# A sparse attention and maxout kernel: emission order from a list scheduler inside the kernel, key tiles in token order, and a first batch masked by matmul

## The chip, the cores, the metric

The kernel runs on one NeuronCore of a Trainium2 chip. The metric is device time in microseconds (us) of one execution; the span of a profile is 1.6 to 2.7 us shorter in these runs, since it goes from the first to the last instruction. The engines are named as in the profile: PE is TensorE (PEld its weight loads), DVE is VectorE, ACT is ScalarE, POOL is GpSimd, SP is SyncE, which here issues the DMAs. A "q" behind an engine's name is its sequencer.

## The reference

Inputs q, k and v are float32 of shape (4, 8, 768, 64): 4 batches, 8 heads, 768 tokens, 64 dims. Cut to what matters:

```python
block, window = 32, 16
k_sum = k.reshape(B, H, nb, block, D).max(axis=3)      # 24 block maxima of k
v_sum = v.reshape(B, H, nb, block, D).mean(axis=3)     # 24 block means of v
scores_l = where(|i - j| < window, scale * q @ k.T, -1e9)
scores_s = scale * q @ k_sum.T + log(block)
a = softmax(concat(scores_l, scores_s))
attn = a @ concat(v, v_sum)
x = attn as (3072 tokens, 512)                          # heads side by side
h1, h2 = x @ w1, x @ w2                                 # 512 -> 1024
out = maximum(h1, h2) @ w_out                           # 1024 -> 512, float32
```

Both kernels use max(h1, h2) = h1 + relu(h2 - h1). So they need `wd = w2 - w1`, and fold the h1 part into `w1o = w1 @ w_out`. No output can be computed before w1o exists, and w1o needs all of w1 and w_out.

## The kernel before

Keys are taken in 12 tiles of 64 queries: 96 nearby keys and the 24 block sums make the 120 rows of one score matmul. Two heads share a matmul (a "head pair"). Cuts are marked with `...`.

```python
def load_pair(src, b, hp, tag):            # k, q or v of two heads: runs of 2 tokens = 512 bytes
    t = stage.tile([128, 6, 128], F32, tag=tag, bufs=3, name=tag)
    nc.sync.dma_start(out=t[:], in_=src[b, 2 * hp:2 * hp + 2].rearrange(
        "h (c p j) d -> p (h c) (j d)", p=128, j=2))
    return t

def prep_v(b):
    ...                                     # cast v to bf16: four DVE copies into vbt
    for j in range(2):
        r = j * 48
        nc.sync.dma_start(out=vx[r:r + 48, 0], in_=vbt[0:48, 0, j])
        ...                                 # 8 DMAs in each turn: rows of v to the key tiles
    ...                                     # matmuls with amean: block means, to vx[96:120, 0]
    nc.sync.dma_start(out=vx[96:NK, 1:NT]..., in_=vx[96:NK, 0:1] broadcast)   # the 17th

def attention(b):                           # a generator: yields between stages
    prep_kq(b, 0)
    yield
    for hp in range(NP):
        scores(b, hp, 0)
        yield
        ...
        values(b, hp, 2)
        yield

def maxout(b):                              # hidden layer in halves of 384 tokens, then output
    ...
            ps = psum.tile([128, d_model], F32, tag="o", bufs=1, name="o_ps")   # one bank
    ...

load_batch(0)
prep_v(0)
load_weights()
for _ in attention(0):
    pass
cast_weights()
make_w1o()
for b in range(B):
    side = iter(())
    if b + 1 < B:
        load_batch(b + 1)
        prep_v(b + 1)
        side = attention(b + 1)
    for _ in maxout(b):                     # one step of attention(b+1) per step of maxout(b)
        next(side, None)
    for _ in side:
        pass
```

The softmax here doesn't subtract the row's maximum and nothing guards it: scores larger than these inputs give would overflow.

## Time and profile before

| | before |
|---|---|
| median of three runs | 225.39 us (225.26 to 226.34) |
| span of the profile | 224.2 us |
| first hidden matmul (L330) | 40.2 us |
| first w1o matmul (L174) | 61.9 us |
| last matmul | 221 us |

First the page of the kernel before: busy time per engine, then the span in 40 slices of 5.6 us, where each digit is the busy share in tenths; PEclk is the granted clock of TensorE.

```profile
PE 174.6 (78%) x1475; PEld 103.8 (46%) x1496; DVE 118.0 (53%) x268; ACT 102.7 (46%) x173; POOL 23.9 (11%) x61
...
PE   0003832665788999896989999999999999999973
...
PEclk9999999997699999999999999999999999999999
DMA  6998438999997335999634599634431101202112
```

PE does nothing in the first three slices and little in the next nine. But "busy" is no measure of matmul work, since a record includes the time in which the matmul waits in the pipeline. The timeline of the dense end gives the real spacing:

```profile
207.00 4.24 PE L330 MATMUL h_ps<-xt,wd 128*128 128x384 bf16 x24
...
213.92 0.59 ACT L347 COPY osb<-o_ps 128x512 f32<-128x512 f32 x1 [2.14 <-PE o_ps L343]
214.55 1.02 PE L339 MATMUL o_ps<-w1o,xt 128*128 128x512 bf16 x4 [0.72 <-ACT osb L347]
```

In the chain of waits the same 24 matmuls take 4.08 us. From the starts of matmuls in such rows I take 216 ns for 512 columns, 163 ns for 384, 56 ns for 128 and 30 ns for the value matmuls, which have 65 (in undisturbed groups they start 30 ns apart in the mean). With one such spacing for each weight load (all 1,496 of them are in the trace), the necessary PE work can be summed by stretch. These sums are estimates; "lost" is the length of a stretch less its work.

| kernel before, us | length | PE work | lost |
|---|---|---|---|
| 0 to 40 | 40 | 5.0 | 35.0 |
| 40 to 75 | 35 | 20.5 | 14.5 |
| 75 to 130 | 55 | 47.8 | 7.2 |
| 130 to 190 | 60 | 55.2 | 4.8 |
| 190 to 221 | 31 | 27.8 | 3.2 |

49.5 of 64.7 lost us lie before 75 us. The tail's losses have a visible reason, in the row at 214.55 above: the output uses one PSUM bank, so PE waits 0.72 us for the copy.

The chain of waits shows why the fill, the time until PE has steady work, is long (columns: start, us, what the chain followed):

```profile
4.46 7.18 DMA vf<-in_v_dram
11.66 1.08 DVE vb_113 L182
12.74 0.55 SPq L127
13.38 6.33 DMA vf<-in_v_dram
19.74 0.57 DVE vb_113 L182
20.36 0.63 SPq L188
...
31.47 0.60 SPq L195
32.18 4.53 DMA vext_115<-vext_115
36.75 0.78 PE av L277 x11
```

v arrives last of three loads per pair, its last cast ends at 20.3 us, then SyncE is occupied by 17 small spreads (the DMAs that copy rows of v to the key tiles) until 33 us, and the first full value group runs at 36.75 us.

### The profile page before, as it was taken

The numbers are of one execution on the slowest core, as the hardware profiler recorded it, in microseconds if no ns is written. First come the engines' busy times: TensorE is split into PE (matmuls) and PEld (weight loads), VectorE is DVE, ScalarE is ACT, GpSimd is POOL, SyncE is SP. The second block draws the span as 40 slices with busy tenths as digits, with TensorE's granted clock in tenths as the row PEclk, the third lists the DMA queues.
The fourth block names the chain that finished last, engine by engine and source line by source line (L and its number), as shares of the span: only waits on it lengthen the run. The fifth ranks groups of instructions, "written<-read, shape, count | busy, mean of one in ns | idle before, by whom it ended". The sixth has DMA issues, their size and how long they took to land.

```text
span 224.2 us, 3831 instructions
## 1 busy us (share of the span) xinstructions
PE 174.6 (78%) x1475; PEld 103.8 (46%) x1496; DVE 118.0 (53%) x268; ACT 102.7 (46%) x173; POOL 23.9 (11%) x61
## 2 busy tenths in 40 slices
PE   0003832665788999896989999999999999999973
PEld 0001622543553655664555466655546664544531
DVE  5432852899972950896857069844727853000000
ACT  2000651575120573585179248824935972442521
POOL 8990110000000010000011001000000000000000
PEclk9999999997699999999999999999999999999999
DMA  6998438999997335999634599634431101202112
GB/s 187 289 290 273 106 100 251 375 365 283 288 281 183 90 90 135 288 292 282 184 117 102 158 259 306 163 116 152 103 87 50 51 0 47 96 0 95 47 47 94
DMA packets 49858, 37.68 MB, mean 168 GB/s; under 512 B 2192, under 2 KB 44720, under 8 KB 49840
## 3 DMA queue, kind: packets, MB, share of 16 engines
q1 hardware_dynamic: 49840, 37.45, 58.5%
q8 instruction: 11, 0.18, 0.3%
q14 instruction: 7, 0.06, 0.1%
HBM read 25.17 MB, written 6.29 MB: 140 GB/s over the span
## 4 chain that ended last, share of the span: by engine, by line
PE 49%; DMA 15%; DVE 13%; ACT 11%; SPq 7%; issue 3%; POOL 1%; ACTq 0%; POOLq 0%
PE o_ps L343 16%; DMA vf<-in_v_dram 13%; PE h_ps L330 11%; PE o_ps L339 8%; PE av L277 4%; PE sc L253 2%; ACT g L332 2%; PE x_ps L294 2%; DMA vext_115<-vext_115 2%; DVE wd L161 2%; SPq L127 2%; ACT qbd_107 L242 2%; PE vs_ps L199 2%; ACT qbd_108 L242 2%; PE w1o_ps L174 2%
## 5 line engine op out<-in xcount | busy, mean ns | idle before, releaser
L330 PE MATMUL h_ps<-xt,wd 128*128 128x384 bf16 x256 | 54.2, 331 | 2.5 <-DVE xt L296 1.1
L343 PE MATMUL o_ps<-wo,g 128*128 128x512 bf16 x186 | 46.5, 379 | 0.3
L332 ACT ACTIVATE g<-h_ps 128x384 bf16<-128x384 f32 x64 | 30.1, 491 | 15.7 <-PE h_ps L330 15.2
L347 ACT COPY osb<-o_ps 128x512 f32<-128x512 f32 x24 | 14.1, 586 | 49.2 <-PE o_ps L343 49.1
L330 PEld LDWEIGHTS <-wd 128*128 128x128 bf16 x256 | 23.7, 98 | 16.8 <-issue 3.0
L343 PEld LDWEIGHTS <-g 128*128 128x128 bf16 x192 | 17.9, 98 | 18.2
L339 PE MATMUL o_ps<-w1o,xt 128*128 128x512 bf16 x83 | 24.1, 378 | 2.1 <-ACT osb L347 1.4
L199 PE MATMUL vs_ps<-vb_113,amean 128*128 128x512 bf16 x12 | 4.2, 502 | 20.4 <-DVE vb_113 L182 20.4
L282 DVE RECIPROCAL inv<-av 128x6 f32<-128x6 f32 x32 | 6.1, 190 | 25.0 <-PE av L277 24.9
L284 DVE TENSOR_TENSOR x<-av,inv 128x384 bf16<-128x384 f32 x32 | 17.6, 550 | 0.3
L234 DVE TENSOR_REDUCE ks<-k_ps 128x24 bf16<-128x768 bf16 x16 | 15.1, 945 | 0.0
L162 ACT CAST wo<-wof 128x1024 bf16<-128x1024 f32 x4 | 4.2, 1043 | 23.8 <-DMA wof<-in_moe_w_out_dram 23.8
L339 PEld LDWEIGHTS <-xt 128*128 128x128 bf16 x96 | 9.1, 97 | 10.4 <-issue 4.0
L199 PEld LDWEIGHTS <-amean 128*128 128x128 bf16 x24 | 2.5, 107 | 24.3 <-issue 13.8
L296 DVE COPY xt<-x_ps 128x384 bf16<-128x384 bf16 x32 | 11.3, 352 | 2.8 <-PE x_ps L294 2.2
L294 PE MATMUL x_ps<-identity,x 128*128 128x128 bf16 x96 | 11.2, 230 | 1.4 <-ACT qbd_108 L242 0.6
L242 ACT COPY qbd_107<-q_ps 64x768 bf16<-64x768 bf16 x10 | 7.9, 792 | 9.3 <-PE q_ps L219 9.2
L255 ACT ACTIVATE prob_109<-sc,bias 120x512 bf16<-120x512 f32 x12 | 8.3, 689 | 7.8 <-PE av L277 6.7
L242 ACT COPY qbd_106<-q_ps 64x768 bf16<-64x768 bf16 x12 | 9.5, 793 | 4.0 <-PE q_ps L219 3.9
L213 DVE CAST qb<-qf 128x768 bf16<-128x768 f32 x16 | 10.3, 647 | 1.1 <-DMA qf<-in_q_dram 1.1
L182 DVE CAST vb_113<-vf 128x768 bf16<-128x768 f32 x8 | 5.1, 638 | 10.4 <-DMA vf<-in_v_dram 10.3
L219 PE MATMUL k_ps<-identity,kb 128*128 128x128 bf16 x96 | 9.8, 236 | 1.0 <-DVE ks L234 0.9
(94 smaller groups left out, 251.0 us busy)
## 6 DMA issues: line engine op xcount, KB each, us to landing
kf<-in_k_dram SPq DMA_DIRECT2D x16, 384.0 KB
qf<-in_q_dram SPq DMA_DIRECT2D x16, 384.0 KB
vf<-in_v_dram SPq DMA_DIRECT2D x16, 384.0 KB
out_dram<-osb SPq DMA_DIRECT2D x24, 256.0 KB
w1f<-in_moe_w_dram SPq DMA_DIRECT2D x4, 512.0 KB
wof<-in_moe_w_out_dram SPq DMA_DIRECT2D x4, 512.0 KB
w2f<-in_moe_w_dram SPq DMA_DIRECT2D x4, 512.0 KB
vext_115<-vb_113 SPq DMA_DIRECT2D x8, 148.5 KB
```

The source lines that it names most:

```text
L199: nc.tensor.matmul(out=ps[:], lhsT=amean[:, c, :], rhs=vbt[:, c, j, :, 0:D], start=(c == 0 and j == 0), stop=(c == 2 and j == 1))
L213: nc.vector.tensor_copy(out=qb[:], in_=by_slot(loads["qf", b, hp]))
L234: nc.vector.tensor_reduce(out=ks[:], in_=kps.rearrange("p j (n g) -> p n j g", g=16), axis=AX.XY, op=ALU.max)
L242: nc.scalar.copy(out=qx[r, :, a * 64:a * 64 + 64].rearrange("p t (g j) -> p t g j", j=2), in_=qps[r].rearrange("p j (t g) -> p t g j", g=32))
L284: nc.vector.tensor_tensor(out=x[:], in0=av[:, :, :, 0:D], in1=inv[:].to_broadcast([128, 3, 2, D]), op=ALU.mult)
L294: nc.tensor.transpose(out=ps[:, u, :], in_=xs[half][:, u].rearrange("p a d -> p (a d)"), identity=identity[:])
L296: nc.vector.tensor_copy(out=xts[b, half][:, hp, :], in_=ps[:].rearrange("p u n -> p (u n)"))
L330: nc.tensor.matmul(out=h[:], lhsT=wd[:, c, f * 128:f * 128 + 128], rhs=xt[:, c, :], start=(c == 0), stop=(c == KC - 1))
L332: nc.scalar.activation(out=g[:, f, :], in_=h[:], func=ACT.Relu)
L339: nc.tensor.matmul(out=ps[:], lhsT=xt[:, c, sl], rhs=w1o[:, c, :], start=(c == 0), stop=False)
L343: nc.tensor.matmul(out=ps[:], lhsT=g[:, f, sl], rhs=wo[:, f, :], start=False, stop=(f == FC - 1))
L347: nc.scalar.copy(out=o[:, u, :], in_=ps[:])
```

## The change

Its intent: every operation is declared with an engine, an assumed duration, the buffers that it reads and writes, and a priority. A small list scheduler simulates the engines, gives each operation its buffer slot and an order of emission, and the kernel is then emitted in just that order (manual scheduling). Beside this, the data layout is new: keys of a tile stand in token order with row groups of 64 + 32 sums + 32; k and q are loaded in runs of 6 tokens (1,536 bytes), v in runs of one (256 bytes); v is spread by 5 DMAs and one for the means in place of 16 and one; all PSUM banks form one pool; the hidden layer goes in groups of 256 tokens. Batch 0 is done group by group over all head pairs, and its mask is added by a matmul with the identity; GpSimd and ScalarE take the casts of batch 0.

The diff, cut to its core:

```diff
+class Ring:        # slots; find() returns a free slot at the modelled time
+class Buf:         # a buffer; its slot is given when its first writer is scheduled
+class Plan:
+    LAG = {"PE": 0.25, "ACT": 0.2, "DVE": 0.15, "POOL": 0.2, "SP": 2.0}
+    ISSUE, DEPTH = 0.55, 4
+    def op(self, engine, us, fn, read=(), write=(), change=(), touch=(), prio=0.0, label=""):
+        ...
+    def run(self):
+        ...                      # at each 0.02 us, each free engine takes its first ready task
+                if e == "SP":
+                    busy[e] = now + self.ISSUE
+                    t.done = max(sent[-1], now + 0.4) + t.us
+                    sent.append(t.done)
+                else:
+                    busy[e] = t.done = now + t.us
+        ...
+        for t in order:
+            t.fn()
...
+    banks = Ring(list(range(8)), {"kq": 2, "sc": 2, "av": 2, "mm": 3})
...
+            op("SP", 1.05, lambda f=f, src=src: nc.sync.dma_start(
+                out=f.ap[:], in_=src[b, 2 * hp:2 * hp + 2].rearrange("h (p j) d -> p h (j d)", j=J)),
...
+            op("SP", 3.45, lambda f=f, n=n: nc.sync.dma_start(
+                out=f.ap[:].rearrange("p h m d -> p (h m) d"),
+                in_=v[b, 4 * n:4 * n + 4].rearrange("h (m r) d -> r (h m) d", r=128)),
...                              # five spreads of v: 1.3, 1.3, 0.65, 0.6 and 0.2 us
+        op(engines[2], 1.2 if engines[2] == "SP" else 1.6, spread_means, read=[mean],
+           write=[vx[b]], prio=prio + 2, label=f"spread means {b}")
...
+            if mask_on == "PE":
+                for i in range(2):
+                    nc.tensor.matmul(out=view()[:, i], lhsT=identity[:], rhs=hide..., start=(i == 0), stop=False)
...
+    def first_attention():
+            prep(0, hp, hp, *FIRST[hp])
+            for grp in range(NG):
+                pbs[hp, grp] = scores(0, hp, grp, (10, 110, 210)[grp] + hp, "PE")
+        for grp in range(NG):
+            for hp in range(NP):
+                values(0, hp, grp, pbs[hp, grp], (20, 120, 220)[grp] + hp)
...
+    make_w1o(450)
+    for b in range(B):
+        for grp in range(NG):
+            maxout(b, grp, 1000 * b + 1500 + 10 * grp)     # attention(b) has 1000 * b
```

## The prediction

> **What bounds the kernel now.** TensorE, after a long fill. The page counts PE busy 174.6 of 224.2 us, yet a matmul's record includes waiting. The timeline's dense end gives real spacing: eight 512-column matmuls in 1.73 us (216 ns), four 384-column ones in 0.65 us (163 ns), eight score matmuls in 0.45 us (56 ns)[...]. This agrees with the Trainium skill, "TensorE: Matmul & The Clock Gate" (part 1: columns ÷ 2.4 GHz plus 2.5 ns). With the page's counts I estimate 160 us of necessary PE work: hidden 42, output 62, w1o 7, w1 transposes 2, block means 5, k/q transposes 11, scores 11, values 15, x transposes 5.
>
> Counted by stretch, only 26 us of that is done by 75 us: 49 us are lost in the fill. From there to the last matmul (221 us) 134 us of work take 146 us: 91% in the mixed stretch, then a tail where one output bank makes PE wait for the copy (0.7 us each). Copy and store take the last 3.5 us.
>
> Why the fill is long (timeline, chain of waits): SyncE issues in order. v loads come third (chain: "vf" 13%); PE idles to 20.4 us for the last v cast; then 17 small spreads hold the queue from 20.4 to 33 us, most weights are issued after that. Values wait for the spread until 36.75. wd appears at 38.6 to 56.5, w1o only after attention 0, at 62 to 75 us.
>
> **What the change does.** PE work hardly changes: masking by PE adds 24 matmuls of 256 columns (an estimate of 2.6 us). DVE loses 12 mask multiplies (0.43 us each) and batch 0's casts; POOL takes casts. k and q come in 1,536-byte runs, not 512; v in 256-byte runs, not 512: slower by the skill's "DMA: Bandwidth & Descriptors" (Specifications: line rate from 512 bytes). Spreads fall from 17 to 6 a batch. Eight PSUM banks are pooled. All is ordered by priority over modelled times.
>
> **Critical path.** Before w1o can start, DMA must bring batch 0 (4.7 MB), 1.2 MB of spreads and 6.3 MB of weights: 12.2 MB at an estimated 310 GB/s (before: slices of 290 with 512-byte rows, up to 375 with weights) is 39 us, so w1o starts near 42 us (before: 62). By then PE can have done attention 0, hidden 0 and w1 transposes: 26 us, so 16 us are lost in the fill: gain 33. Then 136 us remain at some 95%, since attention is preferred, maxout fills, and pure maxout ends it: 143 us against 146: about 4 gained. Tail unchanged.
>
> **Prediction: 188 us**, 178 to 203 in 8 of 10. Faster by over 2%: 0.93; within: 0.04; slower: 0.03.
>
> **What will show it.** Wd subtractions at about 22 to 38 us; first w1o matmul at 38 to 46 us; PE row at 9s from slice 10 (of 40); no long PE idle on v or DMA after 45 us; last 40 us dense at 216 ns without waits on the output copy.
>
> **What would make it wrong.** The order is fixed by modelled durations: if POOL's casts, the 256-byte v loads or the permuted PSUM copies are slower than modelled, in-order queues stall behind them, and the fill grows (200 and more). If dependencies on the shared PSUM tile are coarser than a bank, PE serializes with its evictions (slower than before). If PE holds 98% and batch 1 arrives in time, 178.

## The result, and the profile after

The kernel after takes 200.03 us (median of 4 runs, 199.25 to 200.78), against 225.32 us before (225.0 to 226.34). The ratio is 0.887, with a 95% interval of 0.8826 to 0.8915. Ratios are computed as the mean time of one kernel's runs over that of the other's in the same rounds, so they are not quite the ratio of the medians quoted. Executions over 1.5% slower than the fastest of the same kernel are left out of the means.

The page after, the same rows as before; a slice is 4.9 us here:

```profile
PE 170.1 (86%) x1664; PEld 119.9 (61%) x1664; DVE 104.8 (53%) x286; ACT 113.2 (57%) x173; POOL 25.0 (13%) x40
...
PE   0358629999999984999849999999999999999991
...
PEclk9999985999999996699999999999999999999999
DMA  6999999999999999999999995033020110311203
```

PE starts at 7.9 us and is full from slice 7 on (counted from 1), but for two dents (slices 15 and 16, and 20 and 21). The DMA row, which had gaps before, is full to slice 24, which ends at 118 us. The dense end no longer waits on a copy: each group of matmuls is followed by the next at once (their records overlap).

```profile
184.59 3.66 PE L548 MATMUL banks<-xt,wd 128*128 128x256 bf16 x32
...
188.08 1.89 PE L562 MATMUL banks<-w1o,xt 128*128 128x512 bf16 x8
...
189.81 3.62 PE L569 MATMUL banks<-wo,g 128*128 128x512 bf16 x16
```

The same accounting as before (value matmuls 30 ns each as there; a 256-column matmul 109 ns):

| kernel after, us | length | PE work | lost |
|---|---|---|---|
| 0 to 30 | 30 | 8.3 | 21.7 |
| 30 to 44.6 (first w1o matmul at 44.5) | 14.6 | 12.4 | 2.2 |
| 44.6 to 60 | 15.4 | 15.2 | 0.2 |
| 60 to 75 | 15 | 12.7 | 2.3 |
| 75 to 105 | 30 | 22.5 | 7.5 |
| 105 to 193.5 (last matmul) | 88.5 | 87.8 | 0.7 |

By 75 us the kernel after has lost 26.4 us, and before 49.5: this is 23 of the 27 us by which the span fell. From 75 us to the last matmul it lost 8.2 against 15.2: another 7. The sum of work rose from 156 to 159 us, mostly by the 24 masks. So the change gained by feeding PE earlier and more evenly, not by giving it less to do. The w1o matmuls, which open the way to all output, show the earlier start (count, ns min/median/max, first and last start; before, then after):

```profile
L174 PE MATMUL w1o_ps<-wo,w1t x30: 376/379/390, 61.9 to 74.8; 128*128 128x512 bf16 x30
```

```profile
L532 PE MATMUL banks<-wo,vx x32: 378/379/379, 44.5 to 52.1; 128*128 128x512 bf16 x32
```

Where the rest of the loss lies, the waits of PE tell (who waited for whom: us in all, times, longest):

```profile
PE banks L448 <- DMA vx<-vx: 9.0, 3, 3.3
PE banks L347 <- POOL kqb L328: 8.5, 2, 7.9
PE banks L402 <- DVE kx L370: 2.2, 1, 2.2
PE banks L448 <- DMA vx<-vb: 2.0, 1, 2.0
```

The second row is mostly the wait for the first k at the start. The first row is the DMA that copies the block means to the other eleven key tiles. It stops PE in batches 0, 1 and 2, as the timeline of PE shows (in brackets: idle before, and its releaser):

```profile
26.00 0.20 PE L448 MATMUL banks<-vx,pb 128*128 128x65 bf16 x1 [1.96 <-DMA vx<-vb]
28.68 0.98 PE L448 MATMUL banks<-vx,pb 128*128 128x65 bf16 x15 [2.47 <-DMA vx<-vx]
...
76.68 0.98 PE L448 MATMUL banks<-vx,pb 128*128 128x65 bf16 x15 [3.31 <-DMA vx<-vx]
...
101.33 0.39 PE L448 MATMUL banks<-vx,pb 128*128 128x65 bf16 x7 [3.24 <-DMA vx<-vx]
```

The first two stalls cost more than their length. The trace's clock records show half clock from 27.8 to 34.6 us and from 75.6 to 82.4 us, 6.8 us each. The Trainium skill ("TensorE: Matmul & The Clock Gate", part 1) states that PE falls to half clock after an idle window of some 3.4 us, and that these windows run freely, whatever the kernel does. The length agrees: half clock lasts multiples of 3.41 us in every trace, but for a last piece at the end. That the window must be idle throughout does not: in the window from 72.2 to 75.6 us, before the second half clock, PE was idle for 65%. Counted over all 14 traces, each of the 29 windows at full clock with 57% or more idle was followed by half clock, and none of the 619 with 46% or less; between the two both occur. The third stall, 3.24 us before 101.33, fell across two windows (41% and 54% idle) and was not followed by half clock: as to the clock, it had a lucky phase. A stall of 3.3 us at 73.4 us thus became a loss of about 6: 1.6 in the stretch to 75 us, and 4.3 from 75 to 90.

The plan itself, the modelled times in the kernel, can be laid beside the trace, as every PE task stands in the same order in both. The plan ends at 184.4 us, the chip's span at 197.4. The slip of PE against the plan is 1.5 us at the first values of batch 0, 4.3 behind the stall at 28.7, 4.3 to 6.0 from there to 73 us, 8.1 behind the stall at 76.7 and 10.6 behind the half clock, 13.1 behind the stall at 101.3. So, after the start, the plan was missed at three places, all of them arrivals of v, and behind two of them half clock added to the slip; from the last one on PE won back 2 us.

The DMA packets of both traces (each record has a size and a time) tell what changed in the queue's load. "Us of 16 engines" is the sum of the packets' times over 16; packets of one engine can overlap (the DMA share reaches 1.09 in some stretches), so this is a measure of load and not of time.

| packets | before: ns each, us of 16 engines | after: ns each, us of 16 engines |
|---|---|---|
| k and q | 512 B: 31.0, 47.6 | 1,536 B: 72.9, 37.3 |
| v | 512 B: 31.0, 23.8 | 256 B: 22.2, 34.1 |
| spreads of v and means, 1,056 B | 68.3, 24.2 | 85.8, 32.3 |
| w1 and w2 | 4,096 B: 178.9, 11.5 | 1,024 B: 52.8, 13.5 |
| w_out and output, 2,048 B | 89.3, 22.9 | 90.0, 23.0 |
| sum, the smallest packets included | 131.2 | 141.4 |

What k and q gain from long runs, v loses with short ones, and the spreads are dearer although they are fewer DMAs. In a fill where DMA is full, this is 10 us more of DMA work.

### The profile page after: what moved, and what is told of

The parts are those of the page before. It is cut to its first block, busy times and chain, and to the rows that moved or that the text cites. A ratio compares the mean times of both kernels' runs of the same rounds, so it can differ in the third digit from the quotient of the medians.

```text
span 197.4 us, 4172 instructions
## 1 busy us (share of the span) xinstructions
PE 170.1 (86%) x1664; PEld 119.9 (61%) x1664; DVE 104.8 (53%) x286; ACT 113.2 (57%) x173; POOL 25.0 (13%) x40
## 4 chain that ended last, share of the span: by engine, by line
PE 76%; DMA 11%; POOL 3%; DVE 3%; ACT 2%; issue 2%; SPq 1%; POOLq 0%; ACTq 0%
PE banks L569 20%; PE banks L548 19%; DMA vx<-vx 11%; PE banks L562 10%; PE banks L448 7%; PE banks L402 5%; PE banks L347 4%; PE banks L532 3%; PE banks L302 3%; PE banks L472 3%; PE banks L391 2%; DVE kx L361 1%; POOL hide L229 1%; PE banks L504 1%; SPq L294 1%
## 5 line engine op out<-in xcount | busy, mean ns | idle before, releaser
L548 PE MATMUL banks<-xt,wd 128*128 128x256 bf16 x384 | 47.5, 276 | 0.1
L569 PE MATMUL banks<-wo,g 128*128 128x512 bf16 x192 | 46.5, 379 | 0.0
L414 ACT ACTIVATE pb<-banks,bias 128x512 bf16<-128x512 f32 x48 | 31.7, 686 | 17.2 <-PE banks L402 16.8
L553 ACT ACTIVATE g<-banks 128x512 bf16<-128x512 f32 x48 | 28.5, 597 | 13.3 <-PE banks L548 11.5
L448 PE MATMUL banks<-vx,pb 128*128 128x65 bf16 x384 | 20.5, 201 | 11.0 <-DMA vx<-vx 9.0
L376 ACT COPY qx<-banks 64x768 bf16<-64x768 bf16 x32 | 25.3, 791 | 7.8 <-PE banks L347 6.3
L448 PEld LDWEIGHTS <-pb 128*128 128x128 bf16 x384 | 17.9, 103 | 14.5 <-issue 6.5
L562 PE MATMUL banks<-w1o,xt 128*128 128x512 bf16 x96 | 24.3, 390 | 0.0
L402 PE MATMUL banks<-qx,kx 128*128 128x128 bf16 (+2 forms) x208 | 18.7, 230 | 2.4 <-DVE kx L370 2.2
L347 PEld LDWEIGHTS <-kqb 128*128 128x128 bf16 x192 | 13.0, 103 | 12.2 <-POOL kqb L328 8.6
L462 DVE TENSOR_TENSOR xs<-banks,inv 128x256 bf16<-128x256 f32 x48 | 18.8, 414 | 0.2
L328 POOL CAST vb<-vf 128x1536 bf16<-128x1536 f32 x8 | 11.8, 1471 | 49.5 <-DMA vf<-in_v_dram 32.2
L460 DVE RECIPROCAL inv<-banks 128x4 f32<-128x4 f32 x48 | 7.9, 174 | 18.8 <-PE banks L448 18.5
L361 DVE COPY kx<-banks 128x768 bf16<-128x768 bf16 x16 | 15.2, 952 | 4.5 <-PE banks L347 4.4
```

The costliest lines, as they stand in the source:

```text
L328: {"DVE": nc.vector.tensor_copy, "ACT": nc.scalar.copy, "POOL": nc.gpsimd.tensor_copy}[engine](out=o, in_=i)
L347: nc.tensor.transpose(out=bank(ps, S, BF16)[:, 128 * j:128 * j + 128], in_=src.ap[:, j].rearrange("p h d -> p (h d)"), identity=identity[:])
L361: op("DVE", 0.9, lambda: nc.vector.tensor_copy(out=kt()[:, :, 0:64], in_=order(kps)), read=[kps], write=[kx[b, hp], kmain], prio=prio, lab ...
L376: op("ACT", 0.8, lambda a=a, r=r: nc.scalar.copy(out=qx[b, hp].ap[r, a, :], in_=order(qps)[r]), read=[qps], write=[qx[b, hp]], prio=prio, ...
L402: nc.tensor.matmul(out=o[:, :, n0:n1], lhsT=w, rhs=qx[b, hp].ap[:, :, c:c + n1 - n0], start=(mask_on != "PE"), stop=(mask_on != "PE" or (i ...
L414: op("ACT", 0.7, lambda: nc.scalar.activation(out=pv(), in_=bank(ps).rearrange("p (i w q) -> p i w q", w=2, q=64), func=ACT.Exp, bias=bias ...
```

## The experiments

Four theories were to be told apart. A: DMA throughput is missing in the first 120 us, above all because of v in 256-byte runs. B: only the small DMA of the means is late. C: the waits are an accident, and PE loses elsewhere. D: PE, which runs its fixed order, stands behind value matmuls that the scheduler placed too early, because its durations of DMAs are too short. Later E: the spreads wait in line behind loads on one queue. Each time is a median with its range; the kernel before was run in the same rounds and took 225.5 to 225.8 us in all of them.

### x1_means_dve: the means copied by VectorE

```diff
-    load_v(0, 0.5, ("POOL", "POOL", "SP"))
+    load_v(0, 0.5, ("POOL", "POOL", "DVE"))
-        load_v(b, 1000 * b - 480, ("POOL", "POOL", "SP"))
+        load_v(b, 1000 * b - 480, ("POOL", "POOL", "DVE"))
```

> The changed kernel, with one part moved: the block means of v are copied to the other eleven key tiles by VectorE (from the first tile, SBUF to SBUF) in place of a DMA of 363 KB, for all four batches. Theory A (the missing time is DMA throughput: the 16 DMA engines are busy without a break to 120 us, and v and its spreads are the heavy part): the page's DMA share falls by 6 to 8 us of all engines, values of batches 0, 1 and 2 start earlier by 1 to 4 us each but still wait, now for the spread of v itself; time 195 to 198 us. Theory B (only the small DMA of the means is late, since it is issued last and stands behind others): all three waits of PE vanish (9 us) and time is 188 to 192. Theory C (the waits are an accident of the order and PE loses elsewhere): 199 to 201.

Measured: 196.06 us (195.39 to 196.68), ratio 0.8682 (0.865 to 0.8713), result correct. PE's waits on v's DMAs fell from 11.0 to 0.3 us, but PE now waits for the keys that VectorE places (2.2 us in the kernel after):

```profile
PE banks L402 <- DVE kx L370: 10.0, 6, 3.2
...
PE banks L448 <- DMA vx<-vb: 0.3, 1, 0.3
```

The copy holds VectorE; its group (elements, count, busy us, mean ns):

```profile
L318 DVE COPY vx<-vx 32x5808 bf16<-32x5808 bf16 x4 | 12.7, 3169 | 0.1
```

It takes 3.17 us, and the scheduler's model says 1.6. In batch 0 it runs from 18.8 to 22.0 us, with keys waiting behind it, and PE stands from 21.5 to 24.7. All packets together, the fetches of instructions included, took 134.8 us of 16 engines, down from 142.7, within A's 6 to 8. B's 188 to 192 was missed: taking the waits away was not enough, since a new one came. The time fits A, but the waits do not ("still wait, now for the spread of v itself" was wrong), and the first values of batches 0 to 2 start no earlier: at 28.1, 73.6 and 100.6 us, against 26.0, 73.2 and 97.9.

### x2_v_long_runs: v in runs of 1,536 bytes

```diff
-                out=f.ap[:].rearrange("p h m d -> p (h m) d"),
-                in_=v[b, 4 * n:4 * n + 4].rearrange("h (m r) d -> r (h m) d", r=128)),
+                out=f.ap[:].rearrange("p h m d -> p h (m d)"),
+                in_=v[b, 4 * n:4 * n + 4].rearrange("h (r m) d -> r h (m d)", m=NM)),
```

> The changed kernel, but each partition reads six neighbouring tokens of v in one run of 1,536 bytes per head in place of six runs of 256 bytes (result wrong on purpose: v rows land in other partitions); the same bytes, the same number of instructions, the same order. Theory A (256-byte runs cost DMA time that the fill lacks): the packets of v take some 19 us of 16 engines in place of 34, the DMA row stops being full about 12 to 15 us earlier than 120 us, the waits for the means shrink and the time is 191 to 195 us. Theory B (only the means' DMA is late) and theory C (the order): 198 to 201.

Measured: 191.53 us (189.97 to 192.69), ratio 0.8486 (0.8439 to 0.8534), result wrong as meant. Packets of 1,536 bytes took 72.1 ns, so v's 4,096 took 18.5 us of 16 engines in place of 34.1. The wait on the means fell from 9.0 to 5.0 us:

```profile
PE banks L448 <- DMA vx<-vx: 5.0, 2, 2.8
```

The DMA row is full to 114 us in place of 118, not the 12 to 15 us less that A forecast. The time is what A expects, and neither B nor C gives it: with DMA work alone lighter and the order the same, 8.5 us came back.

### x3_retimed: only the scheduler's DMA durations

```diff
-            op("SP", 1.05, ...            # k or q of a pair
+            op("SP", 1.17, ...
-            op("SP", 3.45, ...            # half of v
+            op("SP", 4.27, ...
-   1.3, 1.3, 0.65, 0.6, 0.2              # five spreads of v
+   2.0, 2.0, 1.0, 0.92, 0.3
-        op(engines[2], 1.2 if ...         # means
+        op(engines[2], 1.85 if ...
-            op("SP", 1.5, ...             # w1, w2 part
+            op("SP", 1.69, ...
-        op("SP", 1.35, ...                # w_out part
+        op("SP", 1.44, ...
```

The new figures are the packet times of the table above, per transfer.

> The changed kernel with only the list scheduler's DMA durations altered to what the trace of the changed kernel shows per transfer when all engines are busy (k or q 1.17 us in place of 1.05, half of v 4.27 for 3.45, w1 or w2 part 1.69 for 1.5, w_out part 1.44 for 1.35, spreads of v and means by half more). No instruction differs, only their order. Theory A (DMA throughput itself is missing): little to gain, 197 to 201 us; the PE waits on the means vanish or shrink since later work is put in front, but the same work is then missing later. Theory D (throughput suffices, the in-order PE stands behind values that the model places too early): the 9 us of waits are filled with maxout and the time is 189 to 194.

Measured: 193.66 us (192.81 to 194.77), ratio 0.8588 (0.8552 to 0.8625), correct. No instruction was added or taken away, and the DMA work did not fall (144.0 us of 16 engines, instruction fetches included, against 142.7), yet 6.4 us came back. The longest waits of PE, of which the third row is the one on the means:

```profile
PE banks L347 <- POOL kqb L328: 7.8, 1, 7.8
PE banks L402 <- DVE kx L370: 3.2, 2, 1.8
PE banks L448 <- DMA vx<-vx: 2.5, 2, 1.3
```

The wait on the means fell from 9.0 to 2.5 us, and the time is in D's range. The plan, run again from the kernel and laid beside the trace, bears D out. In the kernel after, the first values of the four batches start 1.5, 4.5, 9.7 and 12.2 us behind the plan. In x3 they start 2.0, 2.2, 4.1 and 3.3 us before it; that plan ends at 194.6 us, the chip's span at 192.2. A's "little to gain" is refuted, and C, which gave x1 and x2 no gain, with them. x2 and x3 together say that most of the loss is not DMA work as such but PE held in its order behind an arrival that the model had earlier than the chip; either a faster DMA or a truer model removes it.

### x5_flat_model: every duration 0.6 us

```diff
-        t.engine, t.us, t.fn, t.label = engine, us, fn, label
+        t.engine, t.us, t.fn, t.label = engine, 0.6, fn, label
```

> The changed kernel with every operation, DMAs included, given the same 0.6 us in the scheduler's model; priorities, dependencies and buffers as before. If the model's durations carry the gain over the kernel before: 207 to 225 us. If the gain comes from the priorities, the pooled buffers and the cheaper loads, and any reasonable interleaving serves: 198 to 205.

Measured: 248.77 us (248.23 to 250.88), ratio 1.1046 (1.0994 to 1.1097), correct: slower than both kernels, and outside both ranges. By 75 us PE had done 16.7 us of work (estimate as above; the kernel after 48.6), the first w1o matmul came at 71.3 us in place of 44.5. PE's row, over slices of 6.2 us:

```profile
PE   0266445154359993068599758999999999999993
```

The layout, the pooled banks, the loads and the priorities are all still those of the change. Under this one flat model they gain nothing. Which of the false durations does most of the harm, and how far from the chip's they may be, was not tried.

### x4_retimed_dve: x1 and x3 together

```diff
  x3's durations, and x1's ("POOL", "POOL", "DVE") twice; VectorE's copy of the means still at 1.6 us
```

> Both of the helpful edits together: the scheduler knows the measured DMA durations and VectorE copies the block means. Alone they gave 4.0 us (means by VectorE) and 6.4 us (durations) against 200.0. If they recover different losses (DMA time, and PE standing behind misplaced values): 188.5 to 191. If both only took away the same waits for the means: 193 to 195, no better than the durations alone.

Measured: 194.16 us (193.5 to 197.22), ratio 0.8603 (0.8584 to 0.8622), correct. No better than x3. Its profile is of a slow run and is not read here. As it stood, this looked as if both edits had merely removed the same waits. x11 below shows that this reading was wrong.

### x6_mask_dve and x7_pair_major: two parts of the change undone

```diff
 # x6: batch 0's mask on VectorE, as in the other batches
-                pbs[hp, grp] = scores(0, hp, grp, (10, 110, 210)[grp] + hp, "PE")
+                pbs[hp, grp] = scores(0, hp, grp, (10, 110, 210)[grp] + hp, "DVE")
```

```diff
 # x7: batch 0 pair by pair
-            prep(0, hp, hp, *FIRST[hp])
+            prep(0, hp, 20 * hp, *FIRST[hp])
-                pbs[hp, grp] = scores(0, hp, grp, (10, 110, 210)[grp] + hp, "PE")
+                pbs[hp, grp] = scores(0, hp, grp, 20 * hp + 5 + grp, "PE")
-        for grp in range(NG):
-            for hp in range(NP):
-                values(0, hp, grp, pbs[hp, grp], (20, 120, 220)[grp] + hp)
+        for hp in range(NP):
+            for grp in range(NG):
+                values(0, hp, grp, pbs[hp, grp], 20 * hp + 10 + grp)
```

> The changed kernel with batch 0's band mask multiplied by VectorE as in the other batches, in place of the 24 masking matmuls. If the mask on PE is worth having because VectorE is the tighter engine in the fill: slower by 1.5 to 5 us (201.5 to 205). If it only adds PE work (an estimate of 2.6 us in an engine that anyway waits there): 198 to 201, the same within noise.

> The changed kernel with batch 0 done head pair by head pair, as the other batches are, in place of by groups of 256 tokens over all pairs. If doing it by groups feeds the fill with hidden matmuls (the first hidden one was at 36 us): hidden work starts after 47 us, PE loses 3 to 8 us more in the fill, time 203 to 208. If the fill is set by the DMA queue whatever PE does: 199 to 202.

Measured: x6 204.48 us (203.91 to 206.36), ratio 0.9082 (0.9026 to 0.9138); x7 204.06 us (202.46 to 205.98), ratio 0.9028 (0.899 to 0.9066); both correct. Both times lie in the range that the first reading of each forecast, and each part is worth some 4 us. The scheduler made a new order for each, so this is the worth of the part with its order. The first 45 us in stretches (length, then PE, PEld, DVE, ACT and POOL busy with counts; clock, DMA share, GB/s). The kernel after:

```profile
0.00:45.00 45.00, 28.45 (x329) 23.56 (x330) 28.45 (x79) 23.95 (x34) 15.98 (x32) 0.92 1.07 293
```

With the mask on VectorE (x6):

```profile
0.00:45.00 45.00, 23.73 (x289) 19.43 (x290) 32.56 (x91) 23.63 (x32) 17.00 (x32) 0.96 1.07 295
```

Pair by pair (x7):

```profile
0.00:45.00 45.00, 23.36 (x264) 18.42 (x266) 27.91 (x76) 20.46 (x27) 16.15 (x32) 0.89 1.06 289
```

With the mask on VectorE that engine is busy 4 us longer in the fill, and PE has done less: 24 matmuls more on PE were the cheaper way, as PE was idle there. In x7 the hidden matmuls begin only at 52.9 us, behind w1o, as expected; in the kernel after at 36.0.

### x8_before_weights_first: the kernel before, with weights loaded earlier

```diff
 load_batch(0)
-prep_v(0)
 load_weights()
+prep_v(0)
```

> The kernel before, with only the weight loads called ahead of the preparation of v, so that they are not issued behind the 17 small spreads. If the order of issue alone explains the 20 us between the first w1o matmuls (62 us before, 44.7 us after): 210 to 218 us. If the fill of the kernel before is held by its order of attention and casts on VectorE as well, so that earlier weights alone don't help, or the spreads are now late by as much: 222 to 230.

Measured: 235.2 us (234.61 to 237.0), ratio 1.0446 (1.0401 to 1.0492), correct. It is slower than both ranges. The weights are issued earlier, but now SyncE waits for weight buffers to come free, and issues the spreads of v from 33.5 to 46.7 us in place of 20.4 to 33. PE's waits on v's DMAs rose from 4.1 to 18.0 us:

```profile
PE av L277 <- DMA vext<-vb: 9.6, 1, 9.6
PE av L277 <- DMA vext<-vext: 8.4, 1, 8.4
```

One move in one queue exchanges one late arrival for another. It does not show that no better hand order exists.

### x9_spread_act_queue and x10_spread_pool_queue: the spreads on another queue

The base is x3. The six spreads of each batch are issued by ScalarE (x9) or GpSimd (x10). The scheduler models an issue (0.7 or 1.0 us) and a landing (4.5 or 5.0 us).

```diff
-            op("SP", us, lambda ...: nc.sync.dma_start(
+            op("ACT", 4.5, lambda ...: nc.scalar.dma_start(          # x10: "POOL", 5.0, nc.gpsimd
...
-                    busy[e] = t.done = now + t.us
+                    busy[e], t.done = now + t.hold, now + t.us
```

> The kernel with the retimed scheduler (193.7 us), but the six spreads of v and means of each batch are issued from ScalarE's DMA queue, so that they don't stand behind the 2 to 4 MB of loads already issued on SyncE's queue; the scheduler is told that issue holds ScalarE 0.7 us and landing takes 4.5. Theory E (values are late because the spreads wait their turn in one first-in first-out queue): a spread's median landing falls from 8.8 us to about 4 to 5, batch 0's first values start near 24 us, PE waits on spreads are gone, time 187 to 191. Theory A (engines are simply full): landing stays 7 us or more, time 193 to 196, and ScalarE, which now issues, is the later for it.

> The same with the spreads issued from GpSimd's DMA queue, in place of ScalarE's: GpSimd is busy only 13% of the span. Theory E: as above, 187 to 191 us, and unlike the run with ScalarE no cost on a busy engine. Theory A: 193 to 196. If GpSimd's issue itself is slow, it shows as GpSimd held for more than 2 us per spread and later casts of v, 195 or more.

Measured: x9 215.18 us (213.37 to 216.56), ratio 0.9514 (0.9445 to 0.9583); x10 204.8 us (204.28 to 206.62), ratio 0.9087 (0.9039 to 0.9134); both correct. Theory E falls: its landing of 4 to 5 us did not come, and both runs are slower than x3. In the page's list of DMA issues (the last number is the median from issue to landing, us), x3:

```profile
vx<-vb SPq DMA_DIRECT2D x8, 396.0 KB, 8.8
```

From ScalarE's queue (x9):

```profile
vx<-vb ACTq DMA_DIRECT2D x8, 396.0 KB, 7.5
```

From GpSimd's (x10):

```profile
vx<-vb POOLq DMA_DIRECT2D x8, 396.0 KB, 9.5
```

The Trainium skill would lead one to expect this ("DMA: Bandwidth & Descriptors", section "Issuing engines are not separate DMA queues": all run on the same 16 engines and interleave). The landings agree with it: 1.3 us sooner in x9, 0.7 later in x10; on which engines the packets ran was not looked at. Both kernels were given a landing that the chip does not keep (4.5 and 5.0 us), and D's wait came back, against 2.5 us in x3. In x9:

```profile
PE banks L448 <- DMA vx<-vx: 9.5, 2, 5.6
...
PE banks L347 <- ACT kqb L328: 7.5, 5, 5.2
```

In x10:

```profile
PE banks L448 <- DMA vx<-vx: 11.4, 3, 4.6
```

The first values of the four batches start 5.3, 10.4, 21.7 and 20.2 us behind the plan in x9, and 0.3, 4.8, 11.1 and 16.3 in x10. This fits D, but it is no clean test of it: no run gave the model the true landing, and in x9 ScalarE's sequencer is also held by the issue, up to 4.55 us for two DMAs, and PE waits 7.5 us for its casts (2.2 in x3).

### x11_dve_3us: a correct kernel faster than both

```diff
 # x4, with
-        op(engines[2], 1.85 if engines[2] == "SP" else 1.6, spread_means, ...
+        op(engines[2], 1.85 if engines[2] == "SP" else 3.2, spread_means, ...
```

> Retimed scheduler and means copied by VectorE (194.2 us), now with the copy's measured 3.17 us in the model in place of 1.6. If that run gained nothing over the retimed one (193.7) because the model believed the copy to be half as long: 189 to 192. If 12.7 us of VectorE work in the fill cost what 6 to 8 us less of DMA gives: 193 to 195.

Measured: 189.16 us (188.81 to 192.23), ratio 0.8368 (0.8333 to 0.8403), correct. One number in the model, 1.6 to 3.2, is worth 5 us over x4; the instructions are those of x4 in another order. So x4's failure was a false duration and not a gain counted twice. B's 188 to 192 is met here too, but only together with the other durations: no run has the means on VectorE at 3.2 us and the DMA durations of the kernel after, so B alone was not tested. This kernel beats the kernel after by 10.9 us. Its profile fell in a slow run (192.23 us), so only its time is used.

### x12_v_long_retimed: long runs and a model that knows of them

```diff
 # x3, with x2's access to v (wrong result on purpose), and
-            op("SP", 4.27, ...
+            op("SP", 2.31, ...
```

> The retimed scheduler (193.7 us) with v read in 1,536-byte runs (result wrong on purpose) and told so (2.31 us for half of v). If DMA throughput in the fill is what still separates the kernel from its plan, less DMA work pays again where the order is right: 186 to 190. If retiming had already hidden what the 256-byte runs cost (191.5 for the long runs alone): 191 to 194.

Measured: 190.79 us (190.49 to 192.48), ratio 0.8461 (0.8413 to 0.8508). It lies between the two ranges and in neither, 2.9 us below x3; the 0.7 below x2 is within the noise. So of the 8.5 us that the 256-byte runs seemed to cost in x2, about 3 are left when the order is made for them: the rest was the order.

### The runs side by side

One estimate orders them: the PE work done by 120 us (the spacings above, for each weight load in the trace). In the kernel after PE is dense from there on.

| run | DMA work less | model truer | PE work by 120 us | median us |
|---|---|---|---|---|
| kernel after | | | 86.1 | 200.03 |
| x1 | means | no | 89.7 | 196.06 |
| x3 | no | DMA | 91.3 | 193.66 |
| x2 | v | no | 92.6 | 191.53 |
| x12 | v | DMA | 92.8 | 190.79 |
| x11 | means | DMA and copy | (slow run) | 189.16 |
| x7, x10 | no | | 81.4, 78.6 | 204.06, 204.8 |
| x9 | no | landing false | 75.3 | 215.18 |

## Why the prediction was right, and where it was off

The prediction forecast 188 us (178 to 203) and 0.93 for faster by over 2%. Measured were 200.03 us: inside the range, 12 us above the centre, with 25 of the forecast 37 us gained.

- "TensorE, after a long fill", and the gain in the fill: right. 23 of 27 us of the span came before 75 us (accounting of both traces).
- "PE work hardly changes": right, 156 us before and 159 after by the estimate; the added masks are 2.6 us of it. But the prediction's 160 us held 15 for the 384 value matmuls, at 39 ns each (a spacing that the trace does not show); at the 30 ns between their starts it is 11.5.
- "First w1o matmul at 38 to 46 us": 44.5 us. The estimate of 310 GB/s was near: 293 in the first 45 us.
- "Wd subtractions at about 22 to 38 us": 30.9 to 41.0. The forecast was 3 to 9 us too early.
- "PE row at 9s from slice 10", "last 40 us dense without waits on the output copy": right, apart from the two dents.
- "By then PE can have done attention 0, hidden 0 and w1 transposes: 26 us, so 16 us are lost in the fill": this is the step that failed first. By 44.6 us PE had done 20.8 us and lost 23.9: the w1 transposes and all values of attention 0 were done, but only 48 of the 96 hidden matmuls of batch 0 (the missing half is 5.2 us), and w1o came 2.6 us later than the 42. I took for granted that attention 0 runs while the weights arrive; but its values need v spread over the tiles, and that landed at 28.7 us, with a clock halved until 34.6. The term was 8 us too small.
- "No long PE idle on v or DMA after 45 us": wrong. Two stalls of 3.3 and 3.2 us, at 73.4 and 98.1 us, one of them with half clock behind it, make most of the 9.8 us lost from 60 to 105 us. The forecast for all after w1o was 136 us of work in 143; it was 138 in 149.
- "The order is fixed by modelled durations: if ... the 256-byte v loads ... are slower than modelled, in-order queues stall behind them": this was named as a way to come out at 200 and more, and it is what happened (half of v takes 4.27 us of all engines, modelled 3.45). GpSimd's casts were not to blame (0.83 and 1.47 us, no more than modelled), nor the permuted copies (0.95 for 0.9), and PE's long waits name no eviction of a bank.

So the mechanism was right and the sizes were off: the fill's loss (23.9 for 16 us), the loss from there to the last matmul (10.7 for 7), and some 3 us of tail and launch that I had left out or set low; against these stand 3 us less of PE work than I had summed. That last part is luck: with value matmuls at 30 ns the forecast would have been some 3 us lower, and the miss 15.

Not settled: how the 25 us divide over the parts of the change. x6 and x7 give some 4 us each to the PE mask and to the order by groups, and x5 shows that with one flat duration nothing is gained; the pooled banks, the fewer spreads and the longer k and q runs were not undone one by one. Open too is whether a true model pays or only a cautious one: no run gave the DMAs durations longer than the chip's, and in x3 the chip was already up to 4.1 us ahead of its plan.

## What to carry to other kernels

A static order is only as good as the durations that it was made from: here changes of 7 to 54% in a few DMA durations were worth 6 us, one copy's duration 5 us, and durations that were all alike cost 49. So lay the plan beside the trace, find the places where the slip grows, and correct the model there before changing the kernel. In a fill where the DMA row is full, count packets' times and not bytes, and look at which engine is idle before calling an extra operation on it a cost.

## What the Trainium skill lacked or had wrong

- "DMA: Bandwidth & Descriptors", "Why small descriptors are slow": it gives no rate for short packets. From its 3 cycles of overhead per packet alone, a 256-byte packet would have 0.86 of the rate of a 512-byte one (an estimate from that page: 11 cycles for 256 bytes, 19 for 512). These traces have 22.2 and 31.0 ns, a ratio of 0.70, so the 3 cycles are not all of it.
- The same section says that SBUF to SBUF transfers don't suffer from small packets, and gives a rate for one between cores alone. Here packets of 1,056 bytes took 68 (before) and 86 ns (after) from SBUF to SBUF, against 53 ns for 1,024 bytes from HBM. In x10 the same bytes went in packets of 4,224 bytes, 305 ns each, which is 76 ns for 1,056: so small packets are not the reason. They write 64 or fewer partitions; whether that is the cause was not tried.
- "VectorE: DVE Perf Modes", "Rules for kernel authors": a dense bf16 copy in SBUF would get 4x; a broadcast source is not spoken of there. The copy of 32 x 5,808 bf16 from a broadcast source took 3.17 us; 4 elements per cycle at the stated 0.96 GHz and the page's fixed 150 cycles would be 1.67 (an estimate from that page), 2 per cycle 3.18.
- "TensorE: Matmul & The Clock Gate", part 1, does not say how idle an idle window and how busy a busy one must be. In the 14 traces 57% idle was enough for half clock (29 of 29 windows). Full clock came back after all 35 windows at half clock with 20% idle or less, and after none of the 36 with 26% or more; so it lasted two windows, 6.8 us, behind both stalls of the kernel after, whose first windows were 26% and 32% idle.
- No page says what a stall costs an engine whose order was fixed from too short a duration: 6.4 us of 200 (x3), with the instructions unchanged.
